# Row sums that are checked, a second program behind a branch, and a new written order for TensorE

## The chip, the cores and the metric

The kernel runs on one core of one Trainium2 chip. The metric is the device time of one execution in microseconds (us). The kernel before has a median of 522.92 us over 3 runs (521.4 to 527.8). The profile is of one execution: its span is the time from its first to its last instruction on that core.

Five engines work side by side, each through its own list of instructions: TensorE (PE, matrix products), ScalarE (ACT), VectorE (DVE), GpSimd (POOL) and SyncE (SP, which here issues DMAs). They meet at semaphores.

## The reference

Attention with mixed heads, and a feed-forward network (FFN) with a squared ReLU on its result: 8 batches, 12 heads, 448 positions, 64 values a head.

```python
scores = scale * np.matmul(q, k.transpose(0, 1, 3, 2))
scores = np.einsum('bhij,hg->bgij', scores, w_pre)           # mix the heads before the softmax
scores = scores - np.max(scores, axis=-1, keepdims=True)
attn = np.exp(scores)
attn = attn / (np.sum(attn, axis=-1, keepdims=True) + 1e-09)
attn = np.einsum('bhij,hg->bgij', attn, w_post)              # mix them again after it
x = np.matmul(attn, v)                                       # then heads side by side: 3584 x 768
h = np.maximum(x @ w_in, 0.0)                                # 768 x 2048
out = h * h @ w_out                                          # 2048 x 768
```

q, k and v are normal with deviation 0.1, as are both mixing matrices. So scores are close to 0.

## The kernel before

**The softmax.** The kernel doesn't subtract the maximum. `fn_exp` (L979) takes exp of the mixed scores straight from PSUM and adds up each row on the way (`accum_out`); the row sums land in `rowsum`, a ring of 10 places. DVE takes their reciprocals (L994), and POOL folds these into the weights of the second mix (L1001, `wk2s`). No step looks whether a sum has run over or under.

**The units of TensorE.** All work of TensorE is cut into 950 units, and every unit belongs to one of ten streams, within which the order is fixed:

| Digit | Stream | Line | Tiling of the array |
|---|---|---|---|
| 0 | transposes of q and k | L741, L745 | 64*64 |
| 1 | QK products | L894 | 64*128, the last 64 rows of a batch 64*64 |
| 2 | first mix of heads ("pre") | L963 | 64*64 |
| 3 | second mix ("post") | L1033 | 64*128 |
| 4 | A times V | L1092 | 128*64 |
| 5 | first batch: QK and first mix at once | L842 | 128*128 |
| 6, 7 | first FFN product | L1159 (64*128), for the first two batches L1138 (128*128) | |
| 8, 9 | second FFN product | L1279 (64*128), the last two tiles L1228 (128*128) | |

The first mix works on groups of 10 query rows by 12 heads. So the scores of a tile of QK are copied out of PSUM to `stage`, and SP's DMAs move them from there into the ring `dring`, in another layout (L940).

**The order.** `ORDER` (L29) is a string of 950 digits: each digit says from which stream the next unit comes. So TensorE's order is written out by hand or by a search, and isn't decided while the kernel is built. For the other engines a planner decides: `_Plan.run` (L281) goes through time with the costs that are written at each task, gives each task to the engine that is free first, by priority, and may choose ACT or DVE for copies out of PSUM (`FLEX`). `MODE_SWITCH` (L20) is what the planner counts for a change of tiling, `FETCH` (L23) what it counts until the next block of 256 instructions of TensorE has come. Both only move planned times; no instruction waits for them. Where TensorE would wait early in the program, `warm_up` (L570) puts in matmuls on constants (L582, 128*128).

**The end.** Copies of the last results leave PSUM on ACT and DVE (L459, L460), and SP and ACT send them off (L1251). `emit_engine` (L1418) writes each engine's list of tasks with its waits; SP's last task, `fn_final` (L1381), waits for all output DMAs.

```python
def fn_exp(eng, en):
    return eng.activation(pring[:, pr, 0:S], ps[:, gr.banks[x], 0:S], AF.Exp,
                          accum_out=rowsum[:, pr, :])
```

Of the kernel before, what the change touches and what calls it, by code (L numbers as in the profile page):

```python
# [7 lines left out]
ALU = mybir.AluOpType  # L8
# [11 lines left out]
MODE_SWITCH = 106.0  # L20
ACT_BIAS = 14.5
BLOCK = 256
FETCH = (3200.0, 0.65, 3500.0)  # L23
# [6 lines left out]
    "0010155000555555555555555155511355115531355550055555555333555511352351155552555530203332"  # L30
    "4431100241116731622366733227762372211773367333661124114422266773266113177131673137622266"
    "7722009312933933392002822181833383224412004211811183338311822276762233766111763361322444"
    "2326731176133762116720022673812283383338216124442010267677333776202026771181118133822289"
    "3319111911392229393339224442291631613713711633622007223736221672137600216733702208138111"
    "8333822291911393319222444223831181338313822244422363161373217116316227372020632363371176"
    "2216730027022092393339111911812381318131822244422293193319332922244413831382238631811671"
    "3372261622007337336221672001736222673172001913911193139222838113811382228338313822444444"
    "2281633620027137317263361171622167100277363373362244422183822008118139331922193192291192"
    "2393811933813831382224443226336371117611167222763363621267127733791229393329222883383338"
    "2224442228383787638367367366744477667766767686768676778679989998899988"  # L40
# [278 lines left out]
def bass_talking_heads_attention__then__ffn_squared_relu_kernel(  # L319
# [43 lines left out]
    with ExitStack() as es:  # L363
# [14 lines left out]
        WARM = 60000  # L378
        WSHARE = 0.6
# [12 lines left out]
        rowsum = sb("rowsum", [128, NPS, 1], DT.float32)  # L392
        rinv = sb("rinv", [128, NPS, 1], DT.float32)
        sb("align", [128, 64], DT.uint8)
# [15 lines left out]
        zrow = sb("zrow", [128, S], DT.bfloat16)  # L410
# [19 lines left out]
        sem_last = Sm("olast")  # L430
        sem_out = [Sm("oslot%d" % i) for i in range(NOS)]

        plan = _Plan(NB)

        def c_pe(t):
            return {PE: (t, t + 190.0)}

        def c_ev(cols):
            return {ACT: (cols / 1.2 + 65.0, cols / 1.2 + 175.0),
                    DVE: (cols / 0.96 + 72.0, cols / 0.96 + 160.0)}  # L440

        def add(name, engine, fn, deps, cost, prio, mode=None, group=None, instrs=0):
            return plan.add(name, engine, fn, deps, cost, prio, "ctr", 1, mode, group=group,
                            instrs=instrs)

        events = {}

        def unit(s, name, fn, deps, ns, mode, group, mms):
            kind = name[:2]
            was = events.get(kind, 0.0)  # L450
            events[kind] = was + EVENTS.get(kind, 0.5)
            n = 2 * mms + int(events[kind]) - int(was)
            t = add(name, PE, fn, deps, c_pe(ns), 0, mode, group, n)
            s.append(t)
            return t

        def copy(eng, en, o, i_):
            if en == ACT:
                return eng.activation(o, i_, AF.Copy)  # L459
            return eng.tensor_copy(o, i_)  # L460

        streams = [[] for _ in range(10)]
        plan.streams = streams
        s_T, s_QK, s_pre, s_post, s_AV, s_dir = streams[:6]
        s_F1, s_F2 = streams[6:8], streams[8:]

        def fn_init(eng, en):
            eng.memset(mask[:, :, :], 1.0)  # L470
            eng.memset(wk1[:, :], 0.0)
            eng.memset(wrep[:, :], 0.0)
            eng.memset(wk2b[:, :, :], 0.0)
            return eng.memset(ident[:, :], 0.0)
# [999 lines left out]
```

## Time and profile before

| | |
|---|---|
| Time, median of 3 runs | 522.92 us (521.4, 522.92, 527.8) |
| Span of the profiled execution | 524.4 us |
| Own time of the profiled execution | not printed |
| Instructions in the profile | 23175 |
| PE busy | 510.3 us, 97% |
| ACT busy | 423.3 us, 81% |
| DVE busy | 394.3 us, 75% |
| POOL busy | 199.1 us, 38% |
| Granted clock of PE | 0.999 |
| DMA | 71.85 MB, mean 137 GB/s |

How to read the rows that follow. A row of the timeline gives start and length in us, engine, line, operation, output and inputs, shape, and how many instructions were merged (x16); in brackets stands how long the engine had been idle before it, and what ended that. The start of one unit to the start of the next is the time that a unit takes; the length of a row has the last matmul's whole pipeline in it and overlaps the next. A row of the groups (by line) gives total busy time, mean ns of one, and idle time before them. A row of a table by stretches gives the stretch, its length, then busy time (and count) of PE, weight loads, DVE, ACT and POOL. A row of the chain gives start, length and what it was; "issue" is time in which an engine waited for nothing that the profile shows. A row of the DMA queues gives packets, MB, and the time of the packets as a share of 16 engines; a row of DMA issues ends with the median us from issue to landing.

### The profile page before, as it was taken

How to read it: one execution, taken by the hardware profiler on the slowest of the kernel's cores; microseconds unless marked ns; L12 is line 12 of the kernel's file. 1: busy time of each engine (PE TensorE's matmuls, PEld its weight loads, DVE VectorE, ACT ScalarE, POOL GpSimd, SP SyncE). 2: the span in 40 equal slices, each digit the busy share in tenths (PEclk: the TensorE clock that was granted, in tenths of full speed). 3: DMA queues.
4: the chain of work that ended last, by engine and by line, in shares of the span. 5: the costliest groups of instructions: out<-in, count | busy, mean ns of one | idle time of the engine just before them, and what ended most of it. 6: DMA issues, size and time to landing. Idle time of an engine off the chain costs nothing.

```text
span 524.4 us, 23175 instructions
## 1 busy us (share of the span) xinstructions
PE 510.3 (97%) x9633; PEld 322.6 (62%) x9633; DVE 394.3 (75%) x987; ACT 423.3 (81%) x1218; POOL 199.1 (38%) x391
## 2 busy tenths in 40 slices
PE   7999998999999999999999999999999999999997
PEld 4455766567667565566555665566556565567974
DVE  7965978799888669978998769874788678955430
ACT  3788998989989889888997888988888788786411
POOL 9603454423651365135532456124621333132000
PEclk9999999999999999999999999999999999999999
DMA  9999999746984589646984699547974566541003
GB/s 159 199 215 193 153 195 183 185 90 132 172 177 111 121 183 168 144 89 151 174 159 103 139 182 177 113 90 151 175 113 89 118 154 134 115 101 49 2 22 100
DMA packets 82240, 71.85 MB, mean 137 GB/s; under 512 B 13226, under 2 KB 79514, under 8 KB 82138
## 3 DMA queue, kind: packets, MB, share of 16 engines
q0 software_dynamic: 36624, 32.81, 38.4%
q1 hardware_dynamic: 45226, 37.38, 29.6%
q8 instruction: 77, 1.26, 1.0%
q10 hardware_dynamic: 288, 0.20, 0.1%
q14 instruction: 25, 0.20, 0.1%
HBM read 45.70 MB, written 11.01 MB: 108 GB/s over the span
## 4 chain that ended last, share of the span: by engine, by line
PE 87%; DVE 5%; DMA 4%; ACT 1%; issue 1%; POOL 0%; ACTq 0%; POOLq 0%; DVEq 0%
PE ps L1279 26%; PE ps L1159 18%; PE ps L1033 8%; PE ps L963 7%; PE ps L1138 7%; PE ps L1092 7%; PE ps L894 6%; PE ps L842 5%; DMA dring<-stage 3%; DVE stage L460 2%; PE ps L1228 2%; PE ps L745 2%; DMA kraw<-in_k_dram 2%; DVE a2t L460 1%; ACT pring L980 1%
## 5 line engine op out<-in xcount | busy, mean ns | idle before, releaser
L980 ACT ACTIVATE pring<-ps 128x448 bf16<-128x448 f32 x360 | 191.9, 558 | 17.4 <-PE ps L963 8.7
L1279 PE MATMUL ps<-w_out_sb,h2t 64*128 64x384 bf16 x1664 | 151.8, 323 | 0.7 <-issue 0.6
L1001 POOL TENSOR_TENSOR wk2s<-wk2b,rinv 128x120 bf16<-128x120 bf16 (+1 forms) x179 | 70.7, 398 | 198.6 <-DVE rinv L994 197.8
L460 DVE CAST a2t<-ps 128x480 bf16<-128x480 f32 x194 | 118.6, 640 | 18.9 <-PE ps L1033 17.5
L1159 PE MATMUL ps<-xt,w_in_sb 64*128 64x448 bf16 (+2 forms) x1344 | 122.2, 323 | 1.1 <-issue 1.0
L460 DVE CAST stage<-ps 128x448 bf16<-128x448 f32 (+1 forms) x182 | 109.1, 618 | 11.7 <-PE ps L894 7.7
L1279 PEld LDWEIGHTS ps<-w_out_sb,h2t 64*128 64x128 bf16 x1664 | 77.6, 94 | 51.2 <-issue 4.0
L459 ACT ACTIVATE stage<-ps 128x448 bf16<-128x448 f32 (+1 forms) x178 | 92.2, 558 | 20.2 <-PE ps L894 18.0
L459 ACT ACTIVATE a2t<-ps 128x480 bf16<-128x480 f32 (+1 forms) x174 | 92.5, 577 | 12.6 <-PE ps L1033 11.7
L1159 PEld LDWEIGHTS ps<-xt,w_in_sb 64*128 64x128 bf16 x1344 | 61.4, 94 | 41.9 <-issue 2.5
L980 ACT ACTIVATION_READ_ACCUMULATOR pring<-ps 128x1 f32 x360 | 80.1, 222 | 0.0
L1311 POOL DMA_DIRECT2D out_dram<-osb x52 | 33.7, 653 | 111.1 <-ACT pring L980 62.2
L1033 PEld LDWEIGHTS ps<-wk2s,pring 60*128 60x128 bf16 x2880 | 55.9, 93 | 22.1 <-ACT pring L980 2.5
L1033 PE MATMUL ps<-wk2s,pring 60*128 60x60 bf16 x2880 | 62.3, 187 | 0.4 <-POOL wk2s L1001 0.2
L994 DVE RECIPROCAL rinv<-rowsum 128x2 f32<-128x2 f32 (+1 forms) x184 | 29.1, 158 | 37.1 <-ACT pring L980 36.2
L1200 DVE TENSOR_TENSOR h2t<-h1t 128x448 bf16<-128x448 bf16 (+2 forms) x176 | 52.3, 326 | 6.0 <-ACT h1t L1190 5.7
L1190 ACT ACTIVATE h1t<-ps 128x448 bf16<-128x448 f32 (+2 forms) x91 | 40.1, 451 | 20.6 <-PE ps L1159 15.9
L963 PE MATMUL ps<-dring,wk 64*64 64x448 bf16 (+1 forms) x676 | 52.5, 362 | 2.6 <-DVE rinv L994 1.1
L1191 DVE TENSOR_SCALAR h1t<-ps 128x448 bf16<-128x448 f32 (+2 forms) x85 | 41.7, 496 | 17.0 <-PE ps L1159 9.6
L894 PE MATMUL ps<-qkt 64*128 64x448 bf16 (+1 forms) x360 | 49.4, 354 | 0.2 <-DVE qkt L460 0.2
L1138 PE MATMUL ps<-xt,w_in_sb 128*128 128x220 bf16 (+1 forms) x384 | 41.5, 260 | 1.6 <-ACT stage L459 1.6
L1092 PE MATMUL ps<-a2t,vraw 128*64 128x220 bf16 (+1 forms) x768 | 40.4, 260 | 0.2 <-ACT a2t L459 0.2
(57 smaller groups left out, 416.4 us busy)
## 6 DMA issues: line engine op xcount, KB each, us to landing
dring<-stage SPq DMA_DIRECT2D x309, 105.0 KB
out_dram<-osb POOLq DMA_DIRECT2D x52, 192.0 KB, 3.6
qraw<-in_q_dram POOLq DMA_DIRECT2D x42, 112.0 KB, 5.6
kraw<-in_k_dram POOLq DMA_DIRECT2D x42, 112.0 KB, 5.0
w_in_sb<-in_moe_w_in_dram POOLq DMA_DIRECT2D x8, 384.0 KB, 15.0
vraw<-in_v_dram POOLq DMA_DIRECT2D x24, 128.0 KB
w_out_sb<-in_moe_w_out_dram POOLq DMA_DIRECT2D x8, 384.0 KB, 8.2
vraw<-in_v_dram POOLq DMA_DIRECT2D x24, 96.0 KB
```

The source lines that it names most:

```text
L459: return eng.activation(o, i_, AF.Copy)
L460: return eng.tensor_copy(o, i_)
L894: r_ = eng.matmul(ps[y * w:(y + 1) * w, g.banks[x], 0:S], qkt[r0:r0 + 64, pb, p + y, 0, i0:i0 + w], qkt[r0:r0 + 64, pb, p + y, 1, :], star ...
L963: r_ = eng.matmul(ps[64 * y:64 * y + 64, gr.banks[x], 0:S], wk1[64 * x:64 * x + 64 - R0 * x, :], dring[64 * x:64 * x + 64 - R0 * x, (g0 + ...
L980: return eng.activation(pring[:, pr, 0:S], ps[:, gr.banks[x], 0:S], AF.Exp, accum_out=rowsum[:, pr, :])
L1001: return eng.tensor_tensor(wk2s[:, p0:p0 + n, :], i0.to_broadcast([128, n, PR]), rinv[:, p0:p0 + n, :].to_broadcast([128, n, PR]), ALU.mult)
L1033: r_ = eng.matmul(ps[:, gr.banks[x], o0:o0 + PR], pring[64 * x:64 * x + PR, pr + y, j0:j0 + 2 * PJ], wk2s[64 * x:64 * x + PR, pr + y, :], ...
L1092: r_ = eng.matmul(ps[kk * 64:kk * 64 + 64, g.banks[0], x * n:(x + 1) * n], vraw[:, h, s, :], a2t[half][:, s, h, a0:a0 + n], start=(s == 0) ...
L1138: r_ = eng.matmul(ps[:, g.banks[0], 0:n], w_in_sb[:, ft, t * 128:(t + 1) * 128], xt[:, ft, c0:c1], start=(ft == 0), stop=(ft == NFT - 1))
L1159: r_ = eng.matmul(ps[:, g.banks[x], 0:n], w_in_sb[64 * y:64 * y + 64, ft, t * 128:(t + 1) * 128], xt[64 * y:64 * y + 64, ft, c0:c1], start ...
L1200: return eng.tensor_tensor(h2t[:, t16, o0:o0 + n], h1t[:, s, 0:n], h1t[:, s, 0:n], ALU.mult)
L1279: r_ = eng.matmul(ps[:, g.banks[hh], 0:FH], h2t[64 * y:64 * y + 64, t16, col:col + 128], w_out_sb[64 * y:64 * y + 64, t16, hh * FH:(hh + 1 ...
```

## The change

*The check.* `rowsum` becomes `sums`, with a place of its own for every group of rows of the whole run. After the last exponential DVE takes the largest and the smallest sum of each partition, tests them against 1e30 and 1e-20, and SP moves the 128 results into one row by a DMA; DVE takes the minimum of the row and writes it as an integer to `flag`.

*The branch.* The whole plan moves into `program(safe)`, which runs twice. `program(False)` is the kernel as before plus the check; `program(True)` is a second program, in which the maximum of each row is taken and subtracted before the exponential, without warm-up. After its list of the first program each engine waits for the flag, reads it into a register, and runs the second program if it is below 1. SP keeps its last task, the wait for the outputs, behind the branch.

*The order.* `ORDER` is new. Streams, their units, and the order within a stream stay; the new order has 241 changes of tiling. `MODE_SWITCH` goes from 106 to 102 and `FETCH[0]` from 3200 to 4000 ns.

*Room.* The row of zeros `zrow` has no buffer of its own any more but lies in the output buffer `osb`; the first copies into `osb` wait for the DMA that reads it.

```diff
-MODE_SWITCH = 106.0
+MODE_SWITCH = 102.0
-FETCH = (3200.0, 0.65, 3500.0)
+FETCH = (4000.0, 0.65, 3500.0)
 ORDER = (
-    "0010155000555555555555555155511355115531355550055555555333555511352351155552555530203332"
...
+    "0001155550005555555555555555511355531155550013555555555533355113555113555512555330020320"
...
-        rowsum = sb("rowsum", [128, NPS, 1], DT.float32)
+        sums = sb("sums", [128, B * NCP, 1], DT.float32)
+        nmax = sb("nmax", [128, NPS, 2], DT.float32)
+        test = sb("test", [128, 4], DT.float32)
+        flag = sb("flag", [1, 1], DT.int32)
...
-        zrow = sb("zrow", [128, S], DT.bfloat16)
+        zrow = osb.bitcast(DT.bfloat16)[:, 0, :, :].rearrange("p a b -> p (a b)")[:, 0:S]
...
+        def program(safe):
...
             def fn_exp(eng, en):
+                bias = {"bias": nmax[:, pr, 1:2]} if safe else {}
                 return eng.activation(pring[:, pr, 0:S], ps[:, gr.banks[x], 0:S], AF.Exp,
-                                      accum_out=rowsum[:, pr, :])
+                                      accum_out=sums[:, g, :], **bias)
...
-                t_oe = add("oev%d_%d_%d" % (b, tile, hh), FLEX, fn_oe, [t_o, o_free.get(s)],
+                t_oe = add("oev%d_%d_%d" % (b, tile, hh), FLEX, fn_oe,
+                           [t_o, o_free.get(s, t_z[0])],
...
+            def emit_flag():
+                every = [exp_of[b * NCP + c] for b in range(B) for c in range(NCH)]
+                table = sums[:, :, 0].rearrange("p (b c) -> p b c", b=B)[:, :, 0:NCH]
...
+                def fn_most(eng, en):
+                    return eng.tensor_reduce(test[:, 0:1], table, AX.XY, ALU.max)
+                def fn_least(eng, en):
+                    return eng.tensor_reduce(test[:, 1:2], table, AX.XY, ALU.min)
+                def fn_below(eng, en):
+                    return eng.tensor_scalar(test[:, 2:3], test[:, 0:1], SUM_MOST, None,
+                                             op0=ALU.is_lt)
+                def fn_both(eng, en):
+                    return eng.scalar_tensor_tensor(test[:, 3:4], test[:, 1:2], SUM_LEAST,
+                                                    test[:, 2:3], op0=ALU.is_gt, op1=ALU.mult)
+                def fn_row(eng, en):
+                    eng.dma_start(sums[0:1, 0:128, 0], test[:, 3:4]).then_inc(sem_row.handle, 16)
+                def fn_all(eng, en):
+                    return eng.tensor_reduce(test[0:1, 0:1], sums[0:1, 0:128, 0], AX.X, ALU.min)
+                def fn_flag(eng, en):
+                    return eng.tensor_copy(flag[:, :], test[0:1, 0:1])
+                t = every
+                for n, fn in enumerate((fn_most, fn_least, fn_below, fn_both)):
+                    ns = 480.0 if n < 2 else 80.0
+                    one = add("check%d" % n, DVE, fn, t, {DVE: (ns, ns + 90.0)}, 9e6)
+                    t = t + [one] if n < 2 else [one]
+                t = plan.add("row", SP, fn_row, t, {SP: (1050.0, 2600.0)}, 9e6, sem_row, 16)
+                for fn in (fn_all, fn_flag):
+                    t = add("check%d" % len(plan.tasks), DVE, fn, [t], {DVE: (200.0, 290.0)}, 9e6)
+                return t
...
         def emit_engine(eng_name, eng):
+            tasks = normal[eng_name]
+            last = 1 if eng_name == SP else 0
+            emit(eng_name, eng, tasks[:len(tasks) - last], normal_waits)
+            eng.wait_ge(ctr[DVE].handle, t_flag.semval)
+            good = eng.value_load(flag[0:1, 0:1])
+            with eng.If(good < 1):
+                for s_, v_ in ended:
+                    eng.wait_ge(s_.handle, v_)
+                emit(eng_name, eng, again[eng_name], again_waits)
+            emit(eng_name, eng, tasks[len(tasks) - last:], normal_waits)
```

More of the change, by code (lines that the diff above doesn't have):

```diff
@@ L430, in bass_talking_heads_attention__then__ffn_squared_relu_kernel @@
         sem_last = Sm("olast")
+        sem_row = Sm("row")
         sem_out = [Sm("oslot%d" % i) for i in range(NOS)]
[L433 to L444, printed above, removed]
@@ L462, in bass_talking_heads_attention__then__ffn_squared_relu_kernel @@
[L462 to L474, printed above, removed]
-        t_init = add("init", DVE, fn_init, [], {DVE: (750.0, 850.0)}, -3e6)
@@ L1277, in fn_o @@
                             for y in range(2):
[L1278 removed]
+                                x = ph ^ y
+                                t = t16 + x
                                 r_ = eng.matmul(
[L1280 to L1285 removed]
```

1619 lines of the change are left out of this document (834 added, 785 removed).

## The prediction

> **What bounds the kernel now.** First the page: the span, the busy shares, PE's digits by slice, and the chain that ended last.
>
> ```profile
> span 524.4 us, 23175 instructions
> PE 510.3 (97%) x9633; PEld 322.6 (62%) x9633; DVE 394.3 (75%) x987; ACT 423.3 (81%) x1218; POOL 199.1 (38%) x391
> ...
> PE   7999998999999999999999999999999999999997
> ...
> PE 87%; DVE 5%; DMA 4%; ACT 1%; issue 1%; POOL 0%; ACTq 0%; POOLq 0%; DVEq 0%
> ```
>
> TensorE (PE) is busy from the first slice to the last and makes 87% of the chain, so the time is TensorE's own. PE idles for 524.4 - 510.3 = 14.1 us in all. But "busy" isn't all work, because a change of tiling is counted in it. The timeline of PE alone shows that, where the order changes tiling often:
>
> ```profile
> 101.97 1.48 PE L1279 MATMUL ps<-w_out_sb,h2t 64*128 64x384 bf16 x16
> 103.38 0.38 PE L894 MATMUL ps<-qkt 64*64 64x448 bf16 x4
> 103.69 1.47 PE L1279 MATMUL ps<-w_out_sb,h2t 64*128 64x384 bf16 x16
> 105.00 0.90 PE L1033 MATMUL ps<-wk2s,pring 60*128 60x60 bf16 x48
> ...
> 446.78 0.36 PE L894 MATMUL ps<-qkt 64*64 64x448 bf16 x4
> 446.97 0.36 PE L963 MATMUL ps<-dring,wk 64*64 64x448 bf16 x4
> ```
>
> Read the starts. A unit of L1279 (64*128 tiles) takes 103.38 - 101.97 = 1.41 us when a 64*64 unit follows, and 105.00 - 103.69 = 1.31 us when another 64*128 unit does. A 64*64 unit of L894 takes 0.31 us (103.69 - 103.38) before a 64*128 unit and 0.19 us (446.97 - 446.78) before another 64*64 unit. So a change of tiling costs 0.10 to 0.12 us, and none of it can lie beside other PE work.
>
> The second thing in the PE row is its holes. The 14.1 us begin with what precedes the first matmul and end with what follows the last one:
>
> ```profile
> 1.45 3.67 PE L582 MATMUL ps<-warm 128*128 128x448 bf16 x10 [1.45 <-DVE warm L567]
> L582 PE MATMUL ps<-warm 128*128 128x448 bf16 x17 | 5.5, 470 | 1.6 <-DVE warm L567 1.5
> ...
> 517.77 3.09 PE L1228 MATMUL ps<-w_out_sb,h2t 128*128 128x384 bf16 x18
> 518.81 3.20 SPq L1251 DMA_DIRECT2D out_dram<-osb  x2
> 520.89 0.49 ACT L459 ACTIVATE osb<-ps 128x384 f32<-128x384 f32 x1 [2.11 <-PE ps L1228]
> 521.41 0.64 ACTq L1251 DMA_DIRECT2D out_dram<-osb  x1
> ```
>
> The start is 1.45 us, the end 524.4 - 520.86 = 3.5 us. That leaves 14.1 - 1.5 - 3.5 = 9.1 us of holes in between; warm-up matmuls (5.5 us, of which 3.7 us stand before the first unit) cover 1.8 us more. So a perfect order could win back some 11 us. The larger holes, from the timeline and the chain in order of time:
>
> ```profile
> 73.69 0.38 PE L963 MATMUL ps<-dring,wk 64*64 64x448 bf16 x4 [0.54 <-DMA dring<-stage]
> 77.55 0.38 PE L963 MATMUL ps<-dring,wk 64*64 64x448 bf16 x4 [0.70 <-ACT a2t L459]
> 81.75 1.34 PE L1138 MATMUL ps<-xt,w_in_sb 128*128 128x228 bf16 x12 [1.65 <-ACT stage L459]
> 50.26 0.65 issue
> 276.81 0.57 issue
> 378.18 1.00 issue
> ```
>
> Three are waits for an eviction or a move early in the program, where all sixteen DMA engines are loaded. Three (0.65 + 0.57 + 1.00 = 2.2 us) are "issue": PE stands in the middle of a unit with nothing to wait for. That is what a late block of instructions looks like; the instruction queue is quoted below.
>
> **The change, part by part.**
>
> *Fewer changes of tiling.* Each digit of ORDER takes the next unit of a stream, and each unit has one tiling. Going through both strings gives 256 changes before and 235 after. The warm-up matmuls, 128*128 units put into holes, add five before (from their places in the trace); the total after is stated as 241. So 261 against 241: 20 fewer, at 0.10 us = **-2.0 us**. All of it is on PE's own path. With 15 fewer (256 against 241) it would be -1.5 us; with 0.12 us, -2.4 us.
>
> *The same units in another order.* Streams, units and matmuls are the same 950, so PE's work stays. Units move by 4 places on average, 66 at most. What can change is the 9 to 11 us of holes. Between each producer and consumer I added up unit times and changes of tiling, in both strings. The unit times are those written in the code at the call of each unit; the starts bear them out (1309.6 ns for a unit of L1279, read above as 1.31 us). The shortest distances are alike: from the pre-mix to the post-mix 2.5 us before and 2.3 us after, from the last post-mix to the first A times V 0.6 and 0.7 us. Two are longer after: from the QK product to the pre-mix that needs its moved rows, 7.2 and 8.2 us, and from the transposes to QK, 1.2 and 2.7 us. One is tighter: from A times V to the first FFN product the middle one falls from 2.1 to 1.4 us. These speak for neither side. I take **0 us** for the holes. The bounds are -6 us (half or so of the 11 goes) and +9 us (the holes of the first 85 us, where most waits lie, come twice). Where a hole of those quoted goes, the next thing that is late is the same queue of evictions on ACT and DVE, 81% and 75% busy.
>
> *Checks on DVE.* After the last exponential four operations are added, and two more after a small DMA. The nearest rows:
>
> ```profile
> L460 DVE CAST a2t<-ps 128x480 bf16<-128x480 f32 x194 | 118.6, 640 | 18.9 <-PE ps L1033 17.5
> L994 DVE RECIPROCAL rinv<-rowsum 128x2 f32<-128x2 f32 (+1 forms) x184 | 29.1, 158 | 37.1 <-ACT pring L980 36.2
> ...
> 480.00:490.00 10.00, 10.00 (x238) 9.57 (x236) 5.51 (x18) 6.02 (x15) 1.29 (x2) 1.00 0.17 43
> 490.00:500.00 10.00, 10.00 (x190) 8.95 (x186) 5.29 (x20) 3.23 (x9) 0.00 (x0) 1.00 0.01 3
> ```
>
> Two reductions read 360 values a partition: scaled from the 480-column row, 2 x 0.5 us; four small ones by the RECIPROCAL, 4 x 0.16 us; in all 1.6 us of DVE work. In the two windows (the third busy time is DVE's) DVE works 5.51 and 5.29 us of 10, so idle time hides it. The work added has the lowest priority. The wait is the danger: the fifth operation stands on DVE until the row has come back through a DMA, and behind it stand the ReLUs, squares and evictions that the last FFN units wait for. By the DMA rows
>
> ```profile
> out_dram<-osb SPq DMA_DIRECT2D x6, 96.0 KB, 2.2
> ...
> out_dram<-osb ACTq DMA_DIRECT2D x2, 96.0 KB, 2.5
> ...
> wall<-in_w_pre_dram SPq DMA_DIRECT2D x1, 72.0 KB, 5.4
> ```
>
> a DMA of SP lands after 2.2 us on idle queues (as here, late) and 5.4 us on full ones. The planner sets 2.6 us for it, so DVE stands still for nothing at 2.2 us and for 2.8 us at 5.4. I take **+0.2 us**, bounds 0 and +2.8. SP itself waits for the fourth check before it issues the row; behind it are only the last output DMAs. The row sums now have a place each and the zero row lies in the output buffer: no operation more, a wait on something long done, 0 us.
>
> *The end: a flag and a branch on every engine.* After its last task each engine waits for the flag (long set), reads it from SBUF into a register, compares, and jumps over the second program, which is as long as the first. PE ends at 520.9 us, DVE and POOL earlier. The critical ones are SP and ACT: both issue their last output DMA from 521.41 to 522.05 us, and only then read the flag. Their cover is the landing of that DMA: 521.4 + 2.5 (the ACTq row above) = 523.9 us, so 1.9 us of flag and branch are free. The trace of before shows no register read and no long jump. For the read: between nothing and the 2.2 us of a whole DMA; it's nearest to what one memory request of a sequencer costs, the 0.64 us of the ACTq issue. For the jump: the code after it can't have been streamed in, and the nearest row is the instruction queue:
>
> ```profile
> q8 instruction: 77, 1.26, 1.0%
> ```
>
> 1.0% of 16 x 524.4 us is 84 us, so a 16 KB block takes 1.1 us on its DMA engine alone. From request to use I take the 2.2 us of a DMA of SP; bounds 0 (already there) and 5.0 us (two blocks in turn at 2.5 us). So 0.64 + 2.2 = 2.8 us against 1.9 us of cover: **+1.0 us**, bounds 0 and 2.2 + 5.0 - 1.9 = +5.3.
>
> [...] The 0.6 to 1.0 us "issue" holes in straight code show that late blocks do stop PE here; no run shows a far jump yet.
>
> *Sum.* -2.0 + 0 + 0.2 + 1.0 = -0.8 us. On the profiled execution: 524.4 - 0.8 = 523.6 us of span. That execution's own time isn't printed; its span is 1.5 us above the median of the three runs, 522.92. On that scale: **522.1 us**.
>
> **The rivals.**
>
> *A. The order also closes holes.* For it: 2.7 instead of 1.2 us from the transposes to QK, and 1 us more from QK to the pre-mix, where the 81.75 hole waits for a move. Against it: the tighter FFN starts and the "issue" holes, which depend on where a block's edge falls. With -6 us of holes: 522.1 - 6 = 516 us.
>
> *B. The end becomes the bound (the slower side).* The place is SP and ACT after 522.05 us. If the register read costs a full DMA and the jump needs two blocks, +5.3 instead of +1.0 us: 522.1 + 4.3 = 526.4 us. It decides against the kernel before once read and jump together exceed 1.9 + 1.8 = 3.7 us, since then more is lost than the tilings and checks leave (-2.0 + 0.2). [...]
>
> *C. The new order makes holes.* A QK eviction stuck behind a move, as at 81.75 us, blocks ACT and DVE for 1.65 us at a time. With +9 us: 531 us; over 2% slower needs 10.5 us.
>
> *D. The change doesn't do what it says.* If the flag comes out 0, the second program runs as well: about 1050 us. Scores are near 0, sums near 448 against bounds of 1e-20 and 1e30, and the table leaves out the one column in 46 that nothing writes. Very unlikely.
>
> **How the numbers follow.** Forecast 0.56, A 0.15, B 0.18, C 0.10, D 0.01. The forecast's own range goes from 519 to 525. To hold 8 in 10 the range must reach into A and B and part of C: 516 to 528.5. 2% is 10.5 us, about what a measurement here can tell from no change (the three runs spread over 6.4 us). More than 2% faster means under 512.5: all of the 11 us of holes gone, the far end of A, 0.03. More than 2% slower means over 533.4: the far end of C, C with B, and D, 0.08. Within 2%: 0.89.
>
> **What would show each step.** Starts of units as read above still give 0.10 us for a change of tiling, and PE's busy time falls by about 2 us. PE's idle time stays near 14 us, plus the end. In the timeline of the last 60 us stand six DVE operations on the new tiles, with a gap of some 2 us between the fourth and the fifth. Between the last ACTq issue and the end of the span are 3.4 us instead of 3.0. I'm wrong if that stretch is over 5 us (B), if PE's idle total has moved by over 4 us (A or C), or if "issue" holes of over 1 us stand at many places, since then the longer program feeds PE more slowly.

## The result and the profile after

The changed kernel takes 529.67 us (median of four: 527.47, 529.09, 530.26, 532.7) against 522.91 us for the kernel before: a ratio of 1.0107 with a 95% interval of 1.0067 to 1.0147. In a second comparison it was 530.05 against 523.85 us, ratio 1.0128 (1.0098 to 1.0159). So it is **5.6 to 6.7 us slower**: inside 2%, but 7.6 us above the forecast of 522.1 us and 1.2 us above the top of the range. Where medians and ratios below differ a little, the ratios count, since they leave out executions more than 1.5% above their kernel's fastest; a ratio is turned into microseconds with 523.9 us, the kernel before.

The page of the changed kernel, with the same rows that were shown of the kernel before (the last two are DMA queues and the chain):

```profile
span 524.3 us, 23216 instructions
PE 509.2 (97%) x9631; PEld 322.4 (61%) x9631; DVE 401.7 (77%) x1016; ACT 415.1 (79%) x1195; POOL 198.8 (38%) x391
...
PE   7999999999999999999899999999999999999995
PEclk9999999999999999999899999999999999999999
...
q8 instruction: 79, 1.29, 1.0%
q14 instruction: 31, 0.25, 0.1%
...
PE 92%; ACT 2%; DVE 2%; DMA 1%; issue 1%; POOL 0%; POOLq 0%
```

Three things are to be seen. PE's busy time fell by 1.1 us (510.3 to 509.2). PE's last digit is 5 where it was 7: the end has grown. One digit in the middle is 8, and the granted clock falls in the same slice. PE's idle total is 524.3 - 509.2 = 15.1 us (14.1 before), so in this profile it has not moved by the 4 us that were to show A or C. What is *not* to be seen is the loss itself: the span is 524.3 us, as before (524.4). Two readings clear that up. First, this profile is of the fastest of the four executions (527.47 us), while the profile of before came from one of its slower ones: spans of the kernel before go from 519.7 to 525.4 us with a median of 522.0. Second, time minus span is 527.47 - 524.3 = 3.2 us here. It is 2.9 to 3.2 us in each of the ten executions of the changed kernel, and 1.7 to 2.0 us in every recorded execution of the kernel before (64 in the first two series) and of every variant below. So 1.2 us of the loss lie outside the span, where no row of the page can show them.

The end of the timeline of the changed kernel:

```profile
517.67 0.81 PE L1252 MATMUL ps<-w_out_sb,h2t 128*128 128x384 bf16 x4
518.52 0.49 ACT L466 ACTIVATE osb<-ps 128x384 f32<-128x384 f32 x1 [2.11 <-PE ps L1252]
519.04 0.63 ACTq L1276 DMA_DIRECT2D out_dram<-osb  x1
```

From the last ACTq issue to the end of the span are 524.3 - 519.04 = **5.3 us**, where the kernel before has 524.4 - 521.41 = 3.0. The prediction expected 3.4 and called itself wrong above 5. The reads of the flag, from the rows of the tile `flag` (duration in ns three times, then the start):

```profile
L1513 DVEq TENSOR_LOAD <-flag x1: 739/739/739, 508.0 to 508.0; - x1
L1513 POOLq TENSOR_LOAD <-flag x1: 489/489/489, 509.5 to 509.5; - x1
L1513 PEldq TENSOR_LOAD <-flag x1: 493/493/493, 515.4 to 515.4; - x1
L1513 SPq TENSOR_LOAD <-flag x1: 961/961/961, 519.7 to 519.7; - x1
L1513 ACTq TENSOR_LOAD <-flag x1: 1087/1087/1087, 519.7 to 519.7; - x1
```

DVE, POOL and PE read early, beside the last matmuls. SP and ACT read at 519.7 us, right behind their last issue, and need 0.96 and 1.09 us. The single records of the trace give what follows:

```
SP   read 519.69 (0.96)   compare and branch 520.70 (0.05)   next instruction 523.77
ACT  read 519.72 (1.09)   compare and branch 520.83 (0.05)   next instruction 523.71
output of the last ACTq issue has landed at 522.86
```

The branch itself takes 0.05 us, but the next instruction stands 3.0 us (SP) and 2.8 us (ACT) behind it. Read and jump together are 4.1 us on SP (519.69 to 523.77). In this trace and in both others with the branch at the end (the changed kernel again, and the old order below) a small block of instructions (8 KB) starts 0.92 to 0.95 us behind each of these two branches, which is what fetching the code behind the jump looks like. The landing of the output, meant as cover, comes 3.8 us after its issue (522.86 us) where the kernel before has 2.5 us, and still 0.9 us before SP goes on. So the jump ends last, but the late landing alone would have made the end 1.3 us longer.

The checks, from the rows of the tile `test` of the changed kernel:

```profile
L1354 DVE TENSOR_REDUCE test<-sums x1: 509/509/509, 477.1 to 477.1; 128x1 f32<-128x360 f32 x1
L1357 DVE TENSOR_REDUCE test<-sums x1: 519/519/519, 478.1 to 478.1; 128x1 f32<-128x360 f32 x1
L1360 DVE TENSOR_SCALAR test<-test x1: 148/148/148, 480.0 to 480.0; 128x1 f32<-128x1 f32 x1
L1364 DVE SCALAR_TENSOR_TENSOR test<-test x1: 151/151/151, 480.3 to 480.3; 128x1 f32<-128x1 f32 x1
...
L1371 DVE TENSOR_REDUCE test<-sums x1: 267/267/267, 483.6 to 483.6; 1x1 f32<-1x128 f32 x1
L1374 DVE CAST flag<-test x1: 130/130/130, 484.3 to 484.3; 1x1 int32<-1x1 f32 x1
...
DMA to landing us min/median/max: 2.0/2.0/2.0
```

Six operations, 0.51 + 0.52 + 0.15 + 0.15 + 0.27 + 0.13 = 1.7 us of DVE; the row lands after 2.0 us, and between the fourth and the fifth DVE does other work: ReLUs, squares and a move out of PSUM stand there.

### The profile page after: what moved, and what is told of

The parts are those of the page before. It is cut to its first block, busy times and chain, and to the rows that moved or that the text cites. A ratio compares the mean times of both kernels' runs of the same rounds, so it can differ in the third digit from the quotient of the medians.

```text
span 524.3 us, 23216 instructions
## 1 busy us (share of the span) xinstructions
PE 509.2 (97%) x9631; PEld 322.4 (61%) x9631; DVE 401.7 (77%) x1016; ACT 415.1 (79%) x1195; POOL 198.8 (38%) x391
## 4 chain that ended last, share of the span: by engine, by line
PE 92%; ACT 2%; DVE 2%; DMA 1%; issue 1%; POOL 0%; POOLq 0%
PE ps L1304 26%; PE ps L1183 21%; PE ps L1057 8%; PE ps L970 8%; PE ps L1116 8%; PE ps L1162 7%; PE ps L901 6%; PE ps L849 5%; PE ps L1252 2%; PE ps L752 2%; DMA qraw<-in_q_dram 1%; ACT pring L1003 1%; DVE stage L467 1%; ACT stage L466 1%; PE ps L748 0%
## 5 line engine op out<-in xcount | busy, mean ns | idle before, releaser
L467 DVE CAST a2t<-ps 128x480 bf16<-128x480 f32 (+1 forms) x193 | 118.3, 639 | 20.1 <-PE ps L1057 19.4
L467 DVE CAST stage<-ps 128x448 bf16<-128x448 f32 (+1 forms) x186 | 111.6, 617 | 12.3 <-PE ps L901 7.6
L466 ACT ACTIVATE stage<-ps 128x448 bf16<-128x448 f32 (+1 forms) x174 | 90.7, 551 | 25.1 <-PE ps L901 22.0
L1304 PEld LDWEIGHTS ps<-w_out_sb,h2t 64*128 64x128 bf16 x1664 | 75.9, 94 | 51.9 <-issue 3.0
L1215 DVE TENSOR_SCALAR h1t<-ps 128x448 bf16<-128x448 f32 (+2 forms) x97 | 45.6, 476 | 15.3 <-PE ps L1183 11.4
L1214 ACT ACTIVATE h1t<-ps 128x448 bf16<-128x448 f32 (+2 forms) x79 | 36.4, 468 | 21.5 <-PE ps L1183 18.9
L970 PE MATMUL ps<-dring,wk 60*64 60x448 bf16 (+1 forms) x676 | 51.9, 361 | 0.9 <-DVE h2t L1224 0.4
L1018 DVE RECIPROCAL rinv<-sums 128x2 f32<-128x2 f32 (+1 forms) x184 | 28.8, 157 | 26.5 <-ACT pring L1003 25.9
```

Source lines behind the costliest of these rows:

```text
L970: r_ = eng.matmul(ps[64 * y:64 * y + 64, gr.banks[x], 0:S], wk1[64 * x:64 * x + 64 - R0 * x, :], dring[64 * x:64 * x + 64 - R0 * x, (g0 + ...
L1304: r_ = eng.matmul(ps[:, g.banks[hh], 0:FH], h2t[64 * y:64 * y + 64, t16, col:col + 128], w_out_sb[64 * y:64 * y + 64, t16, hh * FH:(hh + 1 ...
```

## The experiments

Theories at this point: **the end** (rival B: flag and jump on SP and ACT), **the order** (rival C: new holes on PE), **the check**, and **the feed** (a second program of the same length makes PE's own instructions come later). Each part was first done alone.

**One part at a time.** The kernel before again, and the changed kernel again, as the scale:

> The kernel before, unchanged, for a second profile and for the spans of several executions. The changed kernel's time is its span + 3.0 to 3.2 us (527.47 against 524.3, 529.09 against 526.2). If that also holds for the kernel before, the execution profiled first (span 524.4) was one of 527.5 us, its slowest, and the other three had spans near 519.8. Theory S (the first profile was a slow execution): the span of the second profile is 518 to 521 and its 'issue' holes, 2.2 us in the first, are shorter. Rival R (what lies around the span grew with the program): the span is again 524, the time 523.

> The changed kernel, unchanged, beside the kernel before on one chip with more rounds. If the parts add up (old order with branch +2.6 us, new order +1.1 us, checks +1.0 us by the runs so far), it's 4.7 us above the kernel before (0.9%); the first comparison gave 1.07%. Tail in its profile (last matmul's end to the end of the span): 5.8 us as in its first profile, against 3.5 us without a branch.

The old order with all the rest of the change:

```diff
-MODE_SWITCH = 102.0
+MODE_SWITCH = 106.0
-FETCH = (4000.0, 0.65, 3500.0)
+FETCH = (3200.0, 0.65, 3500.0)
-ORDER = (new)
+ORDER = (old)
```

> The changed kernel with the old order and the old two planner constants: check, branch and second program stay. Theory END (the cost is flag and branch after the last output DMA): 2.3 to 2.5 us above the kernel before, about 525.3. Theory FEED (the second program makes all of TensorE's instructions come later): 5 to 7 us above, 528 to 530, with more 'issue' holes than the kernel before. Theory ORDER (the new order costs the rest): as END, 525.3, so some 4 us under the changed kernel.

The same three constants the other way round, in the kernel before:

> The kernel before with the new order and the two new constants alone: no check, no branch, no second program. Theory ORDER: 4 to 5 us above the kernel before, 527. Theory FEED: 2 us under it (fewer changes of tiling), 521. Prediction as it stood: 2 us under it, 521.

The changed kernel without the second program, and without the read and the branch (so the fall-back is left out), once with the new order and once with the old:

```diff
-        again, again_waits, _ = program(True)
...
-            eng.wait_ge(ctr[DVE].handle, t_flag.semval)
-            good = eng.value_load(flag[0:1, 0:1])
-            with eng.If(good < 1):
-                ...
```

> The changed kernel with the check up to the flag, but without reading the flag, without the branch and without the second program; the fall-back for large scores is left out. Theory END with ORDER: 2.3 to 2.5 us under the changed kernel, 527.2. Theory FEED: 6 to 8 us under it, 522 or less. If the DVE checks cost anything, it stands above the kernel with the new order alone by that much: 0.2 us expected.

> Old order and constants, with the check up to the flag but without reading it, without branch and second program (fall-back left out). What the check itself costs: theory CHECK-FREE 0 to 0.3 us above the kernel before; if the 1.0 us between the new order alone and the new order with check is real, +1.0 us. The old order with check and branch was +2.6 us, so under END this is 2.3 to 2.6 us lower than that one.

Measured, each against the kernel before on its own chip:

| Kernel | Order | Check | Branch, 2nd program | Median us | Ratio (95%) | us |
|---|---|---|---|---|---|---|
| before again | old | no | no | 523.76 | 0.9991 (0.9967 to 1.0014) | -0.5 |
| old order, check alone | old | yes | no | 523.47 | 0.9997 (0.9973 to 1.0021) | -0.2 |
| new order alone | new | no | no | 525.02 | 1.0018 (0.9991 to 1.0045) | +0.9 |
| new order, check | new | yes | no | 526.04 | 1.0046 (1.0019 to 1.0074) | +2.4 |
| old order, rest of the change | old | yes | at the end | 526.47 | 1.0056 (1.0029 to 1.0084) | +2.9 |
| changed kernel | new | yes | at the end | 530.05 | 1.0128 (1.0098 to 1.0159) | +6.7 |

The check costs nothing that can be measured behind the old order (-0.2 us, interval -1.4 to +1.1); behind the new one 2.4 - 0.9 = 1.5 us, with both ratios uncertain by about 1.4 us. The new order alone costs 0.9 us where -2 us was forecast, though its interval reaches down to -0.5. The branch and the second program cost 2.9 + 0.2 = 3.1 us behind the old order, and 6.7 - 2.4 = 4.3 us behind the new one. So most of the loss comes with the branch and the second program, and some with the order.

**The branch moved ahead.** Is it the end, or the feed? Here all stays, but ACT reads and branches before its last 8 tasks and SP before its 6 output DMAs; the rest of the first program stands in both arms. Once with the new order, once with the old.

```diff
+        EARLY = {ACT: 8, SP: 7}
...
-            emit(eng_name, eng, tasks[:len(tasks) - last], normal_waits)
+            emit(eng_name, eng, tasks[:first], normal_waits)
             eng.wait_ge(ctr[DVE].handle, t_flag.semval)
             good = eng.value_load(flag[0:1, 0:1])
             with eng.If(good < 1):
+                emit(eng_name, eng, rest, normal_waits)
                 ...
+            with eng.Else():
+                emit(eng_name, eng, tasks[first:], normal_waits)
```

> The changed kernel with the flag read and the branch moved ahead on two engines: on ACT before its last 8 tasks, on SP before its 6 output DMAs; the rest of the first program stands in both arms. Theory END (flag and far jump of SP and ACT after the last output DMA are all that the branch costs): 2.3 to 2.6 us under the changed kernel, and a tail of 3.5 us. Theory FEED (the longer program slows TensorE's instructions): no gain, or under 1 us. ACT stands idle for 4.8 us where the branch goes, more than 1.1 + 2.9 us of read and jump, so no eviction should come later.

> Old order and constants, check, second program, and the branch moved ahead on ACT and SP: the whole function of the changed kernel. END: as the old order with the check alone, 0 to +0.5 us above the kernel before, and at least 4 us under the changed kernel. FEED: +2 us or more above the kernel before.

Measured: new order 525.99 us, ratio 1.0025 (0.9997 to 1.0052), **+1.3 us instead of +6.7**; old order 524.51 us, ratio 1.0024 (1.0005 to 1.0042), +1.3 us instead of +2.9. The reads and the end, new order with the early branch (tile `flag`, then the timeline):

```profile
core 0 of [0], span 521.3 us
...
L1516 SPq TENSOR_LOAD <-flag x1: 482/482/482, 483.7 to 483.7; - x1
L1516 ACTq TENSOR_LOAD <-flag x1: 477/477/477, 499.5 to 499.5; - x1
```

```profile
517.78 0.49 ACT L467 ACTIVATE osb<-ps 128x384 f32<-128x384 f32 x1 [2.11 <-PE ps L1253]
518.30 0.64 ACTq L1277 DMA_DIRECT2D out_dram<-osb  x1
```

The reads lie at 483.7 and 499.5 us, where both engines have idle time, and take 0.48 us each; the end is 521.3 - 518.30 = 3.0 us again, and time minus span is back at 1.8 us. So the end costs 5.3 - 3.0 = 2.3 us in the span (with the old order 2.9) and 1.2 us outside it, 3.5 us of the 5.4 that the move won back (the difference of two ratios, each uncertain by 1.5 us; by the medians it is 4.1). With the old order it won back 1.7 us. Why the 1.2 us outside the span appear in the changed kernel alone, and not with the old order and the same late branch, isn't settled. In both traces of the changed kernel a block of instructions starts 2.4 to 2.6 us behind the end of the span, in the others 1.8 us behind it at the latest or none at all. So a late block for what follows the program would fit; that is argued, not shown.

The feed falls as a main cause: with the second program and an early branch both orders stand at +1.3 us. It adds 1.3 + 0.2 = 1.5 us to the old order and 1.3 - 2.4 = -1.1 us to the new. It isn't ruled out as a small one: for the old order the end alone was to leave at most +0.5 us and the feed +2 or more, and +1.3 lies between.

**What the order does.** Ten profiles, five for each order, show where the saved changes of tiling went. A row of each kind, beside those of before and after: the kernel before again,

```profile
span 523.1 us, 23175 instructions
...
PE 510.5 (98%) x9633; PEld 321.6 (61%) x9633; DVE 394.1 (75%) x987; ACT 423.2 (81%) x1218; POOL 198.6 (38%) x391
```

the new order alone,

```profile
span 523.8 us, 23198 instructions
...
PE 508.2 (97%) x9631; PEld 321.2 (61%) x9631; DVE 400.3 (76%) x1009; ACT 415.3 (79%) x1196; POOL 198.9 (38%) x391
```

and the changed kernel again:

```profile
span 525.3 us, 23216 instructions
...
PE 507.6 (97%) x9631; PEld 321.0 (61%) x9631; DVE 401.6 (76%) x1016; ACT 415.8 (79%) x1195; POOL 198.9 (38%) x391
```

From each page: span, less PE's busy time, less the start (1.45 us), less what follows the last matmul (which ends 0.55 us before the last ACTq issue), leaves PE's holes in between.

| Order | Kernel | PE busy | Holes |
|---|---|---|---|
| old | before; before again; check alone; late branch; early branch | 510.3; 510.5; 510.5; 510.4; 510.2 | 9.1; 7.6; 6.5; 4.9; 3.5 |
| | mean | 510.4 | 6.3 |
| new | changed; changed again; alone; check; early branch | 509.2; 507.6; 508.2; 507.6; 507.7 | 7.8; 10.7; 10.7; 9.2; 8.6 |
| | mean | 508.1 | 9.4 |

PE's busy time falls by 2.3 us with the new order, about what the saved changes of tiling should give: the traces have 261 changes with the old order and 240 with the new, 21 at 0.10 us, and two warm-up matmuls fewer. The holes grow by 3.1 us in the mean. That size is rough, since single profiles of one order differ by up to 5.6 us, and those of the new order are of executions 1.8 us under their kernel's median span on average (0.3 us with the old), so 3.1 is rather too low. The net, +0.8 us, is near what the run with the new order alone measured (+0.9), but neither number is known that well. Part of the new holes are waits that an order sets. In the timeline of PE with the new order alone:

```profile
87.56 0.41 PE L745 MATMUL ps<-ident,qraw 64*64 64x64 bf16 x28 [0.92 <-ACT h1t L1190]
...
89.44 0.41 PE L745 MATMUL ps<-ident,kraw 64*64 64x64 bf16 x28 [0.96 <-DMA kraw<-in_k_dram]
...
322.47 1.31 PE L1159 MATMUL ps<-xt,w_in_sb 64*128 64x448 bf16 x12 [1.73 <-DVE stage L460]
...
258.87 0.40 PE L1033 MATMUL ps<-wk2s,pring 60*128 60x60 bf16 x16 [0.39 <-ACT pring L980]
```

The transposes wait for an eviction and for k itself (0.92 and 0.96 us), an FFN unit waits 1.73 us for a move out of PSUM. The last of these rows (258.87, 0.39 us) is the same place as the largest hole of the changed kernel, in the middle of a unit of the second mix between two FFN units. The changed kernel there:

```profile
253.90 1.32 PE L1183 MATMUL ps<-xt,w_in_sb 64*128 64x448 bf16 x12
255.05 0.40 PE L1057 MATMUL ps<-wk2s,pring 60*128 60x60 bf16 x16
257.86 0.58 PE L1057 MATMUL ps<-wk2s,pring 60*128 60x60 bf16 x16 [2.41 <-issue]
258.26 2.43 PE L1183 MATMUL ps<-xt,w_in_sb 64*128 64x448 bf16 x12
```

and in the profile of the new order with check alone, of the early branch, and of the changed kernel again, one after the other:

```profile
258.75 0.40 PE L1057 MATMUL ps<-wk2s,pring 60*128 60x60 bf16 x16 [0.77 <-ACT a2t L466]
```

```profile
258.80 0.40 PE L1058 MATMUL ps<-wk2s,pring 60*128 60x60 bf16 x16 [1.76 <-issue]
```

```profile
260.89 0.40 PE L1057 MATMUL ps<-wk2s,pring 60*128 60x60 bf16 x16 [1.46 <-ACT a2t L466]
```

Always 16 matmuls of the unit run before the hole and 16 after it. The row of the instruction queue for the stretch from 255.0 to 255.6 us of the changed kernel, just ahead of the hole:

```profile
q8 instruction: 1, 0.02, 10.6%
```

One block of instructions starts there (10.6% of 16 x 0.6 us = 1.0 us), and PE goes on at 257.86 us, 1.3 us or more after its packet has ended.

Counting PE's records settles what such holes are. Take weight loads, matmuls and semaphore instructions in order of start, and count those ahead of each hole of over 0.3 us: 138 holes in the 18 traces. Ahead of 57 of them the count is a multiple of 256 plus 193 or 194, and no other remainder comes up more than 8 times. In 53 of these 57 a 16 KB block starts 2.2 to 2.65 us before PE goes on; of the other 81 holes that is so in 5. So these 57 stand at the ends of PE's blocks, and PE waits there for its next block, whatever releaser their row names. The hole before 257.86 us is one of them (remainder 194), at the same count in all five profiles of the new order. Three of the five rows name a wait for ACT instead; in one of them, with the new order alone, that wait may be real, since ACT's row sum ended only 0.15 us before PE went on.

At this place the hole is 0.39 and 0.77 us without a second program in the kernel, 1.46 to 2.41 us with one. Over all holes of more than 0.3 us at block ends, the five profiles of the old order have 2.2, 0.7, 0.6, 0.5 and 0.6 us and those of the new 4.1, 4.2, 2.2, 0.8 and 3.3 us, in the order of the table. That is 2.0 of the 3.1 us by which the holes grew, and it comes from the three profiles with the new order and a second program (3.3 to 4.2 us); the rest stands elsewhere.

In the changed kernel the hole brings a second loss: the unit behind it takes 2.43 instead of 1.32 us. The table by stretches says why (PEclk is the third value from the end):

```profile
255.00:258.00 3.00, 0.59 (x26) 0.42 (x22) 1.18 (x3) 1.13 (x5) 2.08 (x5) 0.94 0.86 165
258.00:261.40 3.40, 3.40 (x64) 1.97 (x62) 1.33 (x3) 1.25 (x3) 0.48 (x1) 0.56 1.02 208
261.40:266.00 4.60, 4.60 (x108) 2.23 (x104) 4.35 (x11) 3.93 (x12) 0.95 (x3) 1.00 0.63 151
```

For 3.4 us after the hole the granted clock is 0.56 on average, then 1.00 again. The lower clock came here after a hole of 2.4 us; after the 1.76 us of the early branch, above, there was no such stretch (mean granted clock 0.999 in that execution, 0.996 in this one). So the hole cost its 2.4 us and, in the next unit alone, 1.1 us more.

**Are the ends of the blocks at fault?** If so, shifting all of PE's instructions must move the holes and the time. Tiny matmuls (32*32) go in ahead of the first warm-up, in time in which PE would only run warm-up matmuls, with one warm-up matmul fewer for every twelve; each is two instructions. First with the branch ahead: 32, 64 and 96 of them with the new order, 64 with the old.

```diff
+        PAD = 32
...
-                    for _ in range(n):
+                    pad = PAD if now < 2000.0 else 0
+                    for _ in range(pad):
+                        r_ = eng.matmul(ps[0:32, g.banks[0], 0:32], warm[:, 0:32], warm[:, 0:32],
+                                        start=True, stop=True)
+                    for _ in range(n - pad // 12):
```

> New order, check, second program, branch moved ahead on ACT and SP (526.0 us without padding), with 32 tiny matmuls (64 instructions of TensorE) put into the warm-up ahead of the first unit, in place of two of its ten. TensorE waits there for its first input anyway, so they cost no time; but every later 16 KB block of its instructions ends 64 instructions earlier. Theory EDGE (the new order loses its gain in 'issue' holes, which stand where a block ends in a dense stretch): the holes of 0.6 to 1.9 us near 53.6, 203, 257 and 313 us move to other units or go, and their sum, 4.4 to 6.7 us so far, comes to another value between 1 and 7; the time follows it by as much. Rival DEPEND (the holes belong to the order's dependencies): the holes stay at the same units, the time within 1 us of 526.0.

> The same with 64 tiny matmuls: block ends 128 instructions, half a block, earlier. EDGE: no hole where there was one, the sum of 'issue' holes different from that with 32 and without; if the phase is as good as the one that the order has without a second program (1.9 to 2.7 us of such holes), 522 to 523.5 us. DEPEND: 526.0 within 1 us.

> The same with 96 tiny matmuls: block ends 192 instructions, three quarters of a block, earlier. EDGE: again another sum of 'issue' holes, time 521 to 528 with it. DEPEND: 526.0 within 1 us.

> Old order, check, second program, branch moved ahead (524.5 us, 1.0 us of 'issue' holes in its profile), with 64 tiny matmuls ahead. EDGE: its block ends lie well now, so moving them by half a block brings holes: 525 to 527 us. DEPEND: 524.5 within 1 us.

Then without a second program in the kernel, and one smaller shift of the old order:

> The kernel before, with 64 tiny matmuls (128 instructions) ahead of its first unit in place of five warm-ups; no check, no second program. Theory EDGE (the time hangs on where the 256-instruction blocks end within the order): as much slower as the old order with branch moved ahead became by the same padding (+4.9 us), so 527 to 530 us, with 'issue' holes of 5 to 8 us near 52, 100, 114 and 154 us. Rival (only the longer program is sensitive): within 1 us of the kernel before.

> New order alone (no check, no second program; 1.1 us above the kernel before without padding), with 16 tiny matmuls (32 instructions). EDGE: another sum of 'issue' holes, time anywhere from 521 to 528. If the phase is good, 521 to 522: the 2 us that 20 fewer changes of tiling are worth come out. Rival ORDER (the order is slower by its dependencies at any phase): 524 to 526.

> The same with 112 tiny matmuls (224 instructions, so the block ends lie 32 instructions later than without padding). EDGE: 521 to 528, different from the one with 16; ORDER: 524 to 526. The first unit can start up to 0.5 us later, since hardly a full warm-up is left.

> Old order, check, second program, branch moved ahead (1.2 us above the kernel before without padding), with 16 tiny matmuls (32 instructions). EDGE: between the 524.5 us without padding and the 529.4 us with 64 or better than both; a small step moves most block ends within the same unit, so 523 to 527.

The holes (those of over 0.3 us at block ends) and the end (last ACTq issue to the end of the span) are those of the one profile of each kernel, in us. Two of these profiles are of long executions: 532.4 us with 64 tiny matmuls in the old order (its median is 529.42), and 532.18 us with 96 in the new (530.22).

| Base | Tiny matmuls | Ratio (95%) | Holes at block ends | End |
|---|---|---|---|---|
| before (two profiles) | 0 | 1 | 2.2; 0.7 | 3.0; 3.0 |
| | 64 | 1.0016 (0.9982 to 1.005) | 4.8 | 3.0 |
| old order, early branch | 0 | 1.0024 (1.0005 to 1.0042) | 0.6 | 3.0 |
| | 16 | 1.0039 (1.001 to 1.0068) | 4.2 | 4.2 |
| | 64 | 1.0088 (1.0053 to 1.0122) | 6.4 | 4.5 |
| new order alone | 0 | 1.0018 (0.9991 to 1.0045) | 2.2 | 3.0 |
| | 16 | 1.0006 (0.9971 to 1.0042) | 1.7 | 3.0 |
| | 112 | 1.0038 (1.0009 to 1.0067) | 5.8 | 3.0 |
| new order, early branch | 0 | 1.0025 (0.9997 to 1.0052) | 3.3 | 3.0 |
| | 32 | 1.0052 (1.0022 to 1.0081) | 1.6 | 4.8 |
| | 64 | 1.0063 (1.003 to 1.0096) | 4.5 | 3.0 |
| | 96 | 1.0081 (1.005 to 1.0112) | 8.2 | 4.7 |

The clearest case is the old order with the early branch: 64 tiny matmuls in idle time cost 0.0064 x 523.9 = 3.4 us. Its profile, of a long execution, shows where holes come rather than their usual size. The chain in order of time (start, length, what), first unshifted, then shifted by 64:

```profile
96.72 0.26 PE ps L971 x4
96.98 1.41 PE ps L1305 x16
98.38 0.50 PE ps L971 x8
```

```profile
100.05 0.43 PE ps L1310 x3
100.47 2.16 issue
102.64 2.42 PE ps L1310 x13
```

A unit of the second FFN product that ran through in 1.41 us is cut after 3 of its 16 matmuls by 2.16 us with nothing to wait for, and its rest runs slower (13 matmuls in 2.42 us). So the ends of the blocks do cost time, and where they fall decides how much: in each of the four bases the ratio goes up with the holes at block ends, except for the shift by 32. With the kernel before, where 64 were to cost microseconds, the holes at block ends did grow, but its other holes fell from 6.9 and 6.8 us to 1.9, and its time went up by 0.8 us, which isn't distinguishable from none. Its executions spread more widely (522.3 to 536.3 us against 521.4 to 528.6), so a cost isn't excluded either. Only two shifts differ from their base by more than the uncertainty of both ratios: 64 in the old order and 96 in the new.

The shift by 32 points at a second place. The output of the last ACTq issue has landed 2.5 us after it in eleven of the 18 traces, and 3.7 to 4.3 us after it in seven. These seven are just those in which a 16 KB block of the queue q8 starts 0.9 to 1.8 us after that issue; in the others it starts 2.0 us or more after it, or not at all. All three traces with the branch at the end are among the seven, and four of the five shifted ones with the branch ahead. With the shift by 32 the end is 1.8 us longer, and the whole loss 0.0027 x 523.9 = 1.4 us. So a block that is fetched at the wrong moment makes the end longer too, even with the branch moved ahead; that it slows the output's own transfer is argued from the coincidence.

No shift helped either order measurably; the new order showed its 2 us of gain at none of the three phases tried without a second program. No version is measurably faster than the kernel before. The old order with the early branch does everything that the changed kernel does, check and fall-back included, for +0.24% instead of +1.28%, some 5 us less.

**What stays open.** The end (3.5 us) and what the early branch still costs (+1.3 us) make 4.8 of the 6.7 us. The other 1.9 us are within the uncertainty of the two ratios (about 2 us together). If they are real, the larger holes at the ends of blocks in the two profiles of the changed kernel are the candidate (4.1 and 4.2 us). Why the new order together with a second program has larger ones was not settled; a second program isn't needed for them, since 112 tiny matmuls without one give 5.8 us.

## Why the prediction was wrong

- **Changes of tiling, -2.0 us: right.** PE's busy time is 2.3 us lower in the mean of five profiles, with 21 changes fewer in the traces; 0.2 to 0.4 us of it come from two warm-up matmuls that are no longer there.
- **The same units in another order, 0 us: wrong, the first step that failed.** The holes grew by some 3.1 us, a third of the way to the bound of +9 (rival C) and on its side, and 2.0 of it stand at the ends of PE's instruction blocks. The distances between producer and consumer, added up in both strings, "spoke for neither side"; they didn't contain the transposes' wait for k, the evictions behind moves, or the ends of blocks. The prediction had seen the three "issue" holes rightly as late blocks (their remainders are 193 and 194), but took their sum as unchanged. Its list of the larger holes left out one of 1.12 us at 141.3 us.
- **Checks, +0.2 us: right.** 1.7 us of DVE work against 1.6 forecast, a landing of 2.0 against 2.2 us, and -0.2 us (interval -1.4 to +1.1) measured.
- **The end, +1.0 us: the mechanism right, the size wrong, the second step that failed.** The far jump took 2.8 to 3.0 instead of 2.2 us, the reads on SP and ACT 0.96 and 1.09 instead of 0.64 us. Read and jump make 4.1 instead of 2.8 us, over the 3.7 us from which rival B was to decide. Less the cover of 1.9 us that is +2.2 us; the span's end grew by 2.3. The cover was another than forecast as well: the output landed 3.8 instead of 2.5 us after its issue, so even the jump of the forecast would have left the end 1.3 us longer.
- **Left out of the sum: what lies outside the span**, +1.2 us in the changed kernel. The sum was made on the span, with the rest taken as constant.
- **The base.** The profile of before was taken as 1.5 us above the median, from its span. That set a span beside times, which are 1.8 us longer; among spans it is 2.4 us above the median of 522.0. The forecast doesn't suffer, since the step only takes 0.8 us off the median of 522.92. But the slower execution hid the loss in the comparison of two profiles: 524.4 and 524.3 us.
- **The rivals.** A (the order closes holes) is not borne out: no profile of the new order has fewer holes than the mean of the old. D (the second program runs) is refuted: the span is of one program. B forecast 526.4 us and was true in kind; C was true in small. B and C together had been counted only for the far end, over 2% slower; they came together in moderate size, B with 3.5 us and C with 3.1.
- **The sign "longer program feeds PE more slowly"** was half right: holes of over 1 us stand at few places, not many, and the second program by itself, with the branch moved, costs some 1.5 us with the old order and nothing measurable with the new.

Put into the forecast's sum, the measured terms are -2.3 + 3.1 - 0.2 + 2.3 + 1.2 = +4.1 us instead of -0.8; the measurements say 5.6 to 6.7, so 1.5 to 2.6 us of the loss have no term.

## What to carry to other kernels

A check with a branch belongs where each engine is idle anyway, not behind its last task: on the engines that finish last, the read and the jump stand in the open (4.1 us on SP here), and moving them ahead won back 5.4 us of the changed kernel's 6.7 without giving up any of its function (1.7 us with the old order). A written order for the busiest engine is tuned together with where its instruction blocks end, so fewer changes of tiling by themselves (21 here, with +0.9 us) are no gain until the holes have been read again, in several profiles. And compare times, not only spans: two profiles with equal spans hid a loss of 6 us.

## What the runs showed of the hardware

- The branch that jumps over the whole second program took 0.05 us by its own record on SP and ACT, and 2.6 to 3.5 us until the next instruction there, in the three traces with the branch at the end. A block of instructions started 0.92 to 0.95 us behind it.
- Reading one integer from SBUF into a register took 0.48 to 0.50 us on SP, ACT, POOL and PE and 0.68 to 0.74 us on DVE, each reading alone, and 0.96 to 1.09 us where SP and ACT read at the same moment.
- In straight code, before any shift, PE stopped for up to 2.4 us at the end of an instruction block of 256. Most ends of blocks showed no such hole: each trace has 1 to 7 of over 0.3 us, where PE's 19846 records in the changed kernel make 78 blocks. But the holes of 0.4 to 2.4 us add up to 0.5 to 4.2 us in the ten profiles without a shift, as much as two orders differ by.
- After such a hole of 2.4 us PE's granted clock stood at 0.56 on average for 3.4 us.
- The last output DMA of 96 KB landed 2.5 us after its issue, and 3.7 to 4.3 us after it in the seven traces in which a 16 KB block of instructions started 0.9 to 1.8 us behind that issue.
